# Block 0 through two weight pairs first, x kept on chip, norms as whole sums, and a shorter conversion of float64 words

## Chip, cores and metric

The kernel runs on one core of a Trainium2 chip. The metric is the device time of one execution in microseconds; the median of three runs of the kernel before is 1621.31 us (1619.83 to 1624.52).

## What is computed

Attention over 32 packed queries, a second attention of the queries over that result, and then two gated two-layer MLPs on the 4608 tokens:

```python
def _attn_ref(q, k, v, p):            # q, k, v: 8 x 8 x 576 x 64, p: 8 x 8 x 32 x 64, float32
    p_packed = sm_attn(p, k, v)       # softmax(scale * p k^T) v
    return sm_attn(q, p_packed, p_packed)

def _moe_ref(x, w_gate, w_val, w_out):    # x: 4608 x 512; 512 x 1536 twice, 1536 x 512, float64
    g = x @ w_gate
    return (g * (1.0 / (1.0 + np.exp(-g))) * (x @ w_val) @ w_out).astype(np.float32)

def _moe2_ref(x, w_in, w_out):            # 512 x 2048, 2048 x 512, float64
    h = x @ w_in
    g = np.where(h >= 1, h, np.where(h <= -1, 0.0, (h + 1) ** 2 / 4))
    return (g @ w_out).astype(np.float32)
```

## The kernel before

**Order of the work.** Every operation is handed to a planner (`Order`, lines 43 to 249) with a cost for each engine that can do it, what it reads and writes, and a due time. The planner plays the five engines and one DMA channel through and emits the instructions in the order in which it starts them: it gives each free engine the waiting operation with the earliest due time, and takes TensorE's work from a window of 32 in program order. So costs and due times that are changed at one place move instructions everywhere. DMAs are all issued on the SyncE queue. Buffers come from pools (38 "op" tiles, 4 "raw", 4 "h", 8 PSUM banks "ps" and others); most are handed out in the order in which they were asked for.

**Attention.** Two pairs of heads make a "quad", two quads a batch of 576 tokens, 16 quads in all. `load` (658) and `load_q` (678) bring the inputs; `stage_a` (705) makes the first scores (L697) and their exponentials (L718), `stage_b` (728) the packed result (L741, L760, L788) and its norm, which goes over the partitions with two small matmuls (L799, L807); `stage_c` (832) does the second softmax, and `stage_d` (876) the outputs (L886), which are scaled out of PSUM with a copy (L378 or L382) into an "op" tile and sent to `xT` in HBM.

**Weights.** They are float64. `from_words` (419) turns 512 of them into float32: one ScalarE pass over the upper words (L427), and on VectorE a mask that keeps the sign (L430), a merge of it with the lower words (L434) and a join (L438). `convert_w1` (595) and `prepare_w1` (622) do this for the first MLP, take squares (L391, L393), sum them over the partitions with a matmul against ones (L637) and reduce to the largest (L642); the result is the power of two by which the weights are scaled before they are split into two float16 parts (`split_quarters`, 501; sums and differences on L364). `convert_chunk` (1132) and `prepare_w2` (1175) do the same for the second MLP (L1154, L1161) and keep its weights in HBM in between.

**The MLPs.** Nine blocks of 512 tokens. A unit (`first_unit`, 1392) is the first product of one block with one pair of 128 hidden columns: seven steps of 12 matmuls with 256 columns (L1110). Its second product is added up per block (`second_products`, L1248, for the first three pairs, 24 matmuls of 512 columns to a pair; `second_strassen`, L1366, else). `PHASES` (532) sets which blocks go through which pairs in turn, and `block_x` (1576) where x of a block comes from: for a pair other than the first it is read back from HBM (`fetch_x`, 1218), for the first it is loaded (`load_x`, 1187), scaled and split (`split_x`, 1207). Block 0 needs batch 0 alone (quads 0 and 1), block 1 batches 0 and 1 (quads 0 to 3). `LATE`, `NEXT` and `SPACE` (903 to 905) place the conversions and the quads between the units, two places to a unit.

Of the kernel before, what the change touches and what calls it, by code (L numbers as in the profile page):

```python
# [20 lines left out]
SIGN = -0x80000000  # L21
# [21 lines left out]
class Order:  # L43
# [8 lines left out]
    PATIENCE = {"exp": 0.0}  # L52
    WINDOW = 32
# [72 lines left out]
    def run(self):  # L126
# [34 lines left out]
        def start(op, eng):  # L161
# [9 lines left out]
            else:  # L171
                end = now + op.costs[eng]
# [8 lines left out]
        while issued < len(self.ops) or finishing:  # L181
# [71 lines left out]
def packed_attention_then_two_mlps(ctx, tc, qT, kT, v, pT, w1, wo, w2, wo2, out):  # L253
# [52 lines left out]
    a2s = const.tile([128, 2 * U2], I32, name="a2s")  # L306
    top1 = const.tile([128, U1 + G1], F32, name="top1")
# [5 lines left out]
    kp = const.tile([128, B * NQUAD, 3], I32, name="kp")  # L313
# [105 lines left out]
    def from_words(words, dst, r, w, n):  # L419
# [3 lines left out]

        def bits():
# [76 lines left out]
    def split_quarters(raw, scale, op, key, left, wait_sum=0.0, wait_lo=0.0):  # L501
        base = lambda: raw.t[:, 0:4, :]
        copy(1024, base, base, q(raw, 0, 1, 2, 3) + [key], q(raw, 0, 1, 2, 3), scale=scale)
# [14 lines left out]
    def sums(raw, left, wait):  # L518
# [14 lines left out]
        (1, (0, 1), (0, 2)), (1, (1, 2), (0, 2)), (1, (2, 3), (0, 2)), (1, (0, 3), (2, NB)), (1, (3, 6), (0, NB)),  # L533
# [60 lines left out]

    def convert_w1(item):
# [3 lines left out]
        for src in srcs:  # L599
# [5 lines left out]
            for a, b in ((0, 512), (512, 1024)):  # L605
# [11 lines left out]
                from_words(words, dst, [(wb, 0)], q(raw, *range(a // N, (b - 1) // N + 1)), n)  # L617
# [4 lines left out]
    def prepare_w1(item):  # L622
        kind, p = item
        raws = st.pop(("w1", item))
        ps = o.buf("ps")

        def norm():
            for u, (_, sq) in enumerate(raws):
                s = sq()
                if kind == "out":  # L630
                    moving, dst = [s[:, 0:4:3, :], s[:, 1:3, :]], ps.t
                else:
                    moving = [m[:, :, h:h + 128] for m in (s[:, 0:4:3, :], s[:, 1:3, :])
                              for h in (0, 128)]
                    dst = ps.t[:, u * 256:u * 256 + 256]
                for m, mv in enumerate(moving):
                    nc.tensor.matmul(dst, ones, mv, start=(m == 0), stop=(m == len(moving) - 1))  # L637

        pe(0.43 * len(raws), norm, [k for raw, _ in raws for k in q(raw, 4, 5)], [(ps, 0)],
           unit=ps, opens=True)  # L640
        i = p if kind == "in" else U1 + p
        dve(512, lambda: nc.vector.tensor_reduce(top1[:, i:i + 1], ps.t[:, :512], axis=AX.X, op=ALU.max),  # L642
            [(ps, 0)], [("top", 1, i)], 1.5, 0.0)
# [14 lines left out]
    def load(i):  # L658
        b, qd = divmod(i, NQUAD)
        pb = o.buf("pb")  # L660
        kt, vt = [o.buf("op") for _ in range(2)], [o.buf("op") for _ in range(2)]
# [7 lines left out]
        for j, c0, c1 in ((0, 0, 3), (1, 3, 4)):  # L669
            dma(0.2, lambda j=j, c0=c0, c1=c1: flat(vt[j], (c1 - c0) * 4 * D).rearrange(  # L670
                "p (c d) -> p c d", d=4 * D
            ), lambda c0=c0, c1=c1: v[b, 128 * c0:128 * c1, cols].rearrange("(c p) d -> p c d", p=128),
                [], [(vt[j], 0)])
        dma(0.1, lambda: flat(vt[1], 8 * D)[:S - 512, 4 * D:], lambda: v[b, 512:, cols],
            [], [(vt[1], 1)])
        st["in", i] = (kt, vt, pb)
# [28 lines left out]
    def stage_a(i):  # L705
        kt, vt, pb = st["in", i]
# [22 lines left out]
    def stage_b(i):  # L729
        b, qd = divmod(i, NQUAD)  # L730
        vt = st.pop(("in", i))[1]
# [24 lines left out]
        def values():  # L756
            for c, (off, n) in enumerate(CH):
                vc = flat(vt[c // 3], 768)[:n, (c % 3) * 4 * D:]
# [6 lines left out]
        pe(0.92, values, [(a1T, 0), (a1T, 1), (vt[0], 0), (vt[1], 0), (vt[1], 1)], [(pv, 0)],  # L765
# [58 lines left out]
        if qd == NQUAD - 1:  # L824
# [4 lines left out]
            field(lambda: kx1[:, b:b + 1], lambda: topx[:, b:b + 1], [("topx", b)], [("kx1", b)], 2.0)  # L829
        st[i] = (pp, parts, ppT)  # L830

    def stage_c(i):
# [33 lines left out]
        z2 = o.buf("op")  # L866
# [4 lines left out]
        copy(S, lambda: halves(0), lambda: flat(z, S), [(z, 0)], [(z2, 0)])  # L871
# [4 lines left out]
    def stage_d(i):  # L876
        b, qd = divmod(i, NQUAD)
        pp, parts, z2, halves = st.pop(i)
        for j in range(2):
            xs = o.buf("op")  # L880
            for u in range(2):
# [813 lines left out]
```

## Time and profile before

| | before |
|---|---|
| median of three runs | 1621.31 us |
| the profiled execution | 1620.46 us |
| its span | 1618.7 us |
| TensorE busy | 1555.6 us (96%) |
| VectorE busy | 1298.2 us (80%) |
| GpSimd busy | 1167.4 us (72%) |
| ScalarE busy | 989.4 us (61%) |
| mean granted clock of TensorE | 0.984 |

The span is the part of the execution that the trace covers; 1.8 us lie around it. Busy time is the union of an engine's instructions. A busy TensorE is not one at its peak, since the ends of matmuls are modelled; how many matmuls went into a time tells more. The granted clock is the share of TensorE's higher level, 2.4 GHz.

### The profile page before, as it was taken

How to read it: one execution, taken by the hardware profiler on the slowest of the kernel's cores; microseconds unless marked ns; L12 is line 12 of the kernel's file. 1: busy time of each engine (PE TensorE's matmuls, PEld its weight loads, DVE VectorE, ACT ScalarE, POOL GpSimd, SP SyncE). 2: the span in 40 equal slices, each digit the busy share in tenths (PEclk: the TensorE clock that was granted, in tenths of full speed). 3: DMA queues.
4: the chain of work that ended last, by engine and by line, in shares of the span. 5: the costliest groups of instructions: out<-in, count | busy, mean ns of one | idle time of the engine just before them, and what ended most of it. 6: DMA issues, size and time to landing. Idle time of an engine off the chain costs nothing.

```text
span 1618.7 us, 35291 instructions
## 1 busy us (share of the span) xinstructions
PE 1555.6 (96%) x13772; PEld 1290.2 (80%) x13772; DVE 1298.2 (80%) x2104; ACT 989.4 (61%) x1690; POOL 1167.4 (72%) x993
## 2 busy tenths in 40 slices
PE   4778999999999999999999999999999999999999
PEld 2446666776777778888888888888888888888888
DVE  8889998778675647889999899988777898775674
ACT  5767677677665456666666767666554556654541
POOL 5476556475464357778769989988788888886884
PEclk8779999999999999999999999999999999999999
DMA  8776967647337755666776853245433553244422
GB/s 295 244 268 234 334 223 238 199 170 236 133 140 250 265 179 194 233 249 234 262 238 207 303 190 128 102 150 189 160 105 121 186 182 119 102 170 160 150 60 79
DMA packets 147240, 310.86 MB, mean 192 GB/s; under 512 B 18560, under 2 KB 55424, under 8 KB 147072
## 3 DMA queue, kind: packets, MB, share of 16 engines
q1 hardware_dynamic: 147072, 308.60, 55.7%
q8 instruction: 108, 1.77, 0.4%
q14 instruction: 60, 0.49, 0.1%
HBM read 191.76 MB, written 115.74 MB: 190 GB/s over the span
## 4 chain that ended last, share of the span: by engine, by line
PE 85%; DVE 7%; ACT 2%; issue 2%; POOL 2%; DMA 1%; SPq 0%; POOLq 0%; DVEq 0%; ACTq 0%
PE ps L1110 46%; PE ps L1366 27%; PE ps L1248 7%; PE ps L697 2%; PE ps L886 1%; POOL op L364 1%; POOL raw L364 1%; DVE raw L364 1%; DVE raw L438 1%; DVE h L434 1%; DVE ps L1093 0%; ACT op L376 0%; DMA x2T<-acc 0%; DVE h L1093 0%; PE ps L637 0%
## 5 line engine op out<-in xcount | busy, mean ns | idle before, releaser
L1110 PE MATMUL ps<-op,op 128*128 128x256 f16 x7560 | 906.2, 273 | 7.0 <-DVE u L382 2.5
L1110 PEld LDWEIGHTS <-op 128*128 128x128 f16 x7560 | 737.7, 98 | 116.6 <-issue 14.5
L364 POOL TENSOR_TENSOR op<-h,op 128x512 f16<-128x512 f32 (+2 forms) x344 | 419.5, 1238 | 167.0 <-ACT op L376 140.6
L1366 PE MATMUL ps<-op,op 128*128 128x256 f16 x4158 | 513.3, 273 | 0.0
L1366 PEld LDWEIGHTS <-op 128*128 128x128 f16 x4158 | 406.7, 98 | 47.5 <-issue 0.3
L376 ACT CAST op<-h 128x512 f16<-128x512 f32 (+2 forms) x368 | 202.9, 591 | 92.0 <-POOL h L364 36.1
L364 POOL TENSOR_TENSOR raw<-raw 128x256 f32<-128x256 f32 (+1 forms) x169 | 156.2, 938 | 71.0 <-ACT raw L378 43.4
L364 POOL TENSOR_TENSOR h<-h,h 128x512 f32<-128x512 f32 (+1 forms) x160 | 197.9, 1237 | 11.9 <-DVE h L1488 4.3
L1485 ACT ACTIVATE ps<-m,half,f 128x512 f32<-128x512 f32 x144 | 112.3, 780 | 108.0 <-POOL m L1482 61.1
L378 ACT ACTIVATE p<-ps,f 128x512 f32<-128x512 f32 x174 | 118.8, 685 | 95.2 <-PE ps L1110 90.2
L1266 DVE SCALAR_TENSOR_TENSOR acc<-ps,f,acc 128x512 f32<-128x512 f32 x169 | 125.7, 744 | 58.6 <-PE ps L1366 55.8
L364 POOL TENSOR_TENSOR op<-raw,op 128x512 f16<-128x512 f32 (+3 forms) x100 | 157.3, 1593 | 15.7 <-ACT op L376 9.5
L1248 PE MATMUL ps<-op,op 128*128 128x512 f16 x648 | 155.4, 379 | 0.0
L1488 DVE SCALAR_TENSOR_TENSOR h<-ps,f,h 128x512 f32<-128x512 f32 x144 | 106.4, 742 | 32.5 <-ACT ps L1485 32.3
L1093 DVE SCALAR_TENSOR_TENSOR h<-ps,f,p 128x512 f32<-128x512 f32 x126 | 93.5, 743 | 42.5 <-PE ps L1110 37.2
L1248 PEld LDWEIGHTS <-op 128*128 128x128 f16 x648 | 63.0, 98 | 57.2 <-issue 0.9
L364 POOL TENSOR_TENSOR h<-h 128x512 f32<-128x512 f32 x57 | 78.1, 1371 | 26.0 <-DVE h L1457 15.3
L1482 POOL TENSOR_SCALAR m<-h,f 128x512 f32<-128x512 f32 x72 | 61.7, 856 | 48.6 <-ACT ps L1485 28.9
L364 DVE TENSOR_TENSOR op<-h,op 128x512 f16<-128x512 f32 (+1 forms) x79 | 96.7, 1234 | 0.0
L364 POOL TENSOR_TENSOR op<-op,t 128x576 f32<-128x576 f32 x32 | 39.9, 1246 | 71.9 <-DVE t L848 22.5
L378 ACT ACTIVATE u<-ps,f 128x512 f32<-128x512 f32 x87 | 59.6, 685 | 44.9 <-PE ps L1110 44.6
L376 ACT CAST op<-raw 128x512 f16<-128x512 f32 (+3 forms) x126 | 77.5, 655 | 13.9 <-DVE raw L364 6.9
(148 smaller groups left out, 1791.2 us busy)
## 6 DMA issues: line engine op xcount, KB each, us to landing
op<-xsp SPq DMA_DIRECT2D x88, 448.0 KB, 6.2
xsp<-op SPq DMA_DIRECT2D x72, 448.0 KB, 4.2
sums<-acc SPq DMA_DIRECT2D x88, 256.0 KB, 2.7
acc<-sums SPq DMA_DIRECT2D x88, 256.0 KB, 3.6
op<-wsp SPq DMA_DIRECT2D x44, 448.0 KB, 4.8
op<-wsp_out SPq DMA_DIRECT2D x38, 448.0 KB, 5.3
h<-in_w SPq DMA_DIRECT2D x24, 512.0 KB, 5.2
op<-in_kT SPq DMA_DIRECT2D x32, 288.0 KB, 5.3
```

What stands on the lines that cost most here:

```text
L364: lambda e: engine(e).tensor_tensor(dst(), x(), y(), op=op), r, w, late,
L376: nc.scalar.copy(dst(), src())
L378: nc.scalar.activation(dst(), src(), AF.Copy, scale=scale())
L697: nc.tensor.matmul(ps.t[64 * j:64 * j + 64, :H2], left(j), flat(right[j], S)[:, u * H2:(u + 1) * H2])
L1093: psum_dve(T, lambda: nc.vector.scalar_tensor_tensor(dst(), lanes(bank.t), self.r(), lanes(add.t), op0=ALU.mult, op1=ALU.add), [(bank, 0), ...
L1110: nc.tensor.matmul(dst, a, b, start=start, stop=stop, skip_group_check=True)
L1248: nc.tensor.matmul(bank.t, x[:, js], y, start=first and i == 0 and m == 0, stop=last and i == 1 and m == 2,)
L1266: psum_dve(T, lambda: nc.vector.scalar_tensor_tensor(acc.t, bank.t, pw.output()(), acc.t, op0=ALU.mult, op1=ALU.add), r + [(acc, 0)], [(ac ...
L1366: nc.tensor.matmul(bank.t[:, l * N:(l + 1) * N], x, y, start=first and l == 0 and m == 0, stop=last and l == 1 and m == 2, skip_group_chec ...
L1482: o.add({"POOL": 0.85, "DVE": 0.42}, lambda e: engine(e).tensor_scalar(out=lanes(m.t), in0=dst(), scalar1=top(), scalar2=low(), op0=ALU.mi ...
L1485: act(T, lambda: nc.scalar.activation(bank.t, m.t, AF.Square, bias=half_one[:, 0:1], scale=inv()), [(m, 0), (f, 0)], [(bank, 0)], fixed=0.35)
L1488: psum_dve(T, lambda: nc.vector.scalar_tensor_tensor(dst(), lanes(bank.t), top(), dst(), op0=ALU.mult, op1=ALU.max), [(bank, 0), (h, t), ( ...
```

## The change

`PHASES`: the two first blocks go through pairs 0 and 1 one after the other, block 0 first, where both went through pair 0 and then both through pair 1. `block_x` gives a later one of the first three pairs the x operands that the block had for pair 0, where it read them back from HBM.

x of block 0: `stage_d` writes the outputs of the first 512 tokens, scaled for the MLP, into the "raw" tiles on which `split_x` works; the scale is the new fourth column of `kp`, made when both quads of the batch have their norms. Only the last 64 tokens of batch 0 go to `xT`. The copy by DMA and the scaling pass are left out for this block.

`from_words`: the ScalarE function becomes one with two slopes, which leaves the sign in an exponent bit; VectorE shifts the result left by three and joins the lower words.

Norms of the output weights: ScalarE squares with an accumulated sum (`squares`), a small matmul adds up (`sum_of`).

`load` puts the values beside the keys (three "op" tiles in place of four, four DMAs for the values in place of three), and `stage_c` writes the halves of its result over the tile that it has read. The planner issues no DMA while its model of the channel is more than 4 us behind, counts TensorE's work before 140 us 1.18 times, and puts VectorE work marked "shared" off while the port is taken. `LATE` and `NEXT` change, and x of the next part is asked for one unit ahead instead of two for the first three units.

```diff
@@ class Order
+    QUEUED = 4.0
+    EARLY = 140.0, 1.18
+    PORT, AHEAD = 0.1, 5.0
-                end = now + op.costs[eng]
+                end = now + op.costs[eng] * (self.EARLY[1] if eng == "PE" and now < self.EARLY[0] else 1.0)
-                skipped = []
+                if eng == "SP" and channel - now > self.QUEUED:
+                    upcoming.append(channel - self.QUEUED)
+                    continue
+                skipped, second = [], None
...
+                    if second and op.late > second.late + self.AHEAD:
+                        skipped.append(item)
+                        break
...
-                        start(op, eng)
-                        break
+                        if eng == "DVE" and op.shared and port - now > self.PORT:
+                            second = second or op
+                        else:
+                            second = None
+                            start(op, eng)
+                            break
                     skipped.append(item)
+                if second:
+                    start(second, eng)
@@ def from_words
-            dst(), words()[:, :, 1].bitcast(F32), AF.Abs, scale=2.0 ** -112
+            dst(), words()[:, :, 1].bitcast(F32), AF.Prelu, scale=2.0 ** -112, alpha=-2.0 ** 32
         ), r, w, fixed=0.12)
         dve(n // 2, lambda: nc.vector.tensor_scalar(
-            out=words()[:, :, 1], in0=words()[:, :, 1], scalar1=SIGN, scalar2=None,
-            op0=ALU.bitwise_and,
-        ), r, r, fixed=0.0, shared=True)
+            out=bits(), in0=bits(), scalar1=3, scalar2=None, op0=ALU.logical_shift_left,
+        ), w, w, fixed=0.0, shared=True)
         dve(n, lambda: nc.vector.scalar_tensor_tensor(
-            words()[:, :, 0], words()[:, :, 0], 29, words()[:, :, 1],
-            op0=ALU.logical_shift_right, op1=ALU.bitwise_or,
-        ), r, r, fixed=0.06, shared=True)
-        dve(n, lambda: nc.vector.scalar_tensor_tensor(
-            bits(), bits(), 3, words()[:, :, 0], op0=ALU.logical_shift_left, op1=ALU.bitwise_or,
+            bits(), words()[:, :, 0], 29, bits(), op0=ALU.logical_shift_right, op1=ALU.bitwise_or,
         ), r + w, w, fixed=0.06, shared=True)
@@ PHASES
-        (1, (0, 1), (0, 2)), (1, (1, 2), (0, 2)), (1, (2, 3), (0, 2)), (1, (0, 3), (2, NB)), (1, (3, 6), (0, NB)),
+        (1, (0, 1), (0, 1)), (1, (1, 2), (0, 1)), (1, (0, 1), (1, 2)), (1, (1, 2), (1, 2)), (1, (2, 3), (0, 2)), (1, (0, 3), (2, NB)), (1, (3, 6), (0, NB)),
@@ norms
+    def squares(src, keys, acc, key):
+        act(512, lambda: nc.scalar.activation(junk, src(), AF.Square, accum_out=acc), keys, [key], fixed=0.25)
+    def sum_of(cols, keys, dst, key):
+        t, n = o.buf("ps"), cols.shape[-1]
+        pe(0.1, lambda: nc.tensor.matmul(t.t[:, :n], ones32, cols), keys, [(t, 0)], unit=t, opens=True)
+        dve(n, lambda: nc.vector.tensor_reduce(dst, t.t[:, :n], axis=AX.X, op=ALU.add),
+            [(t, 0)], [key], 1.5, 0.0)
...
+        if kind == "out":
+            sum_of(sq1[:, p, :], [("sq1", p, m) for m in range(2)], top1[:, i:i + 1], ("top", 1, i))
@@ stage_b
+            if b == 0:
+                power(lambda: kpx, lambda: kx1[:, 0:1], -1.0, 202.0, [("kx1", 0)], [("kpx", 0)], 2.0)
+                dve(NQUAD, lambda: nc.vector.tensor_scalar_mul(
+                    kp[:, :NQUAD, 3].bitcast(F32), kp[:, :NQUAD, 2].bitcast(F32), kpx.bitcast(F32)
+                ), [("kpx", 0), *(("kp", j, 2) for j in range(NQUAD))],
+                    [("kp", j, 3) for j in range(NQUAD)], 2.0, 0.0)
@@ stage_d
+            if b == 0:
+                raw = st.setdefault(("x", j), o.buf("raw") if qd == 0 else None)
+                line = lambda raw=raw: raw.t[:, 2 * qd:2 * qd + 2, :].rearrange("p a n -> p (a n)")
...
+                if b == 0:
+                    n = min(hi, T) - lo
+                    copy(n, lambda line=line, lo=lo, n=n: line()[:, lo:lo + n],
+                         lambda xo=xo, n=n: xo.t[:, :n], [(xo, 0), ("kp", i, 3)],
+                         q(raw, *range(2 * qd + u, 2 * qd + 2)), 1.0,
+                         scale=lambda: kp[:, i, 3:4].bitcast(F32), psum=True)
+                    lo = max(lo, T)
@@ places
-    LATE = (1, 2, 5, 6, 14, 26, 38, 43, 48, 52)
+    LATE = (0, 0.5, 5, 7, 14, 26, 38, 43, 48, 52)
-    NEXT, SPACE, AHEAD = (0, 0.5, 1.2, 3.4, 6, 8.5, 11), 2.8, 1
+    NEXT, SPACE, AHEAD = (0.2, 0.9, 1.9, 3.9, 6, 8.5, 11), 2.8, 1
@@ split_x, block_x
-            split_quarters(raw, pw.x(), op, (pw.f, 0), False, SUM_WAIT, X_LO)
+            scale = None if layer == 1 and b == 0 else pw.x()
+            split_quarters(raw, scale, op, (pw.f, 0), False, SUM_WAIT, X_LO)
...
+            if (layer, b, (0, 1)) in xops and pairs[0] < PLAIN:
+                xops[key] = xops[layer, b, (0, 1)]
-            elif pairs[0] > 0:
...
-                if k + 2 < len(line):
-                    block_x(*parts[line[k + 2][0]])
+                then = k + (1 if k < NEAR else 2)
+                if then < len(line):
+                    block_x(*parts[line[then][0]])
```

## Rows read from the trace of the kernel before

**Rows 1.** Busy tenths in 40 slices of 40.5 us; PEclk is the granted clock.

```profile
PE   4778999999999999999999999999999999999999
PEclk8779999999999999999999999999999999999999
```

**Rows 2.** Stages: length, busy us of PE, PEld, DVE, ACT, POOL, clock, DMA share, GB/s.

```profile
0.00:70.60 70.60, 37.32 (x303) 19.75 (x303) 57.20 (x184) 43.16 (x92) 39.19 (x40) 0.76 0.77 258
70.60:114.80 44.20, 33.68 (x276) 21.64 (x275) 36.54 (x92) 31.02 (x61) 27.24 (x23) 0.81 0.82 278
114.80:140.00 25.20, 21.64 (x189) 18.08 (x188) 24.00 (x40) 15.94 (x24) 12.50 (x9) 0.98 0.75 268
140.00:260.00 120.00, 113.22 (x1032) 81.68 (x1031) 113.04 (x239) 89.59 (x165) 77.37 (x64) 1.00 0.79 264
260.00:600.00 340.00, 337.58 (x2706) 244.16 (x2705) 233.86 (x412) 213.72 (x361) 181.42 (x152) 1.00 0.58 197
600.00:1619.00 1019.00, 1012.18 (x9276) 904.84 (x9273) 833.51 (x1140) 595.97 (x993) 829.70 (x708) 1.00 0.50 172
```

**Rows 3.** Chain of waits, first 140 us: start us, us, what.

```profile
23.83 0.61 DVE h L434
...
26.54 1.44 DVE h L434
```

**Rows 4.** ScalarE in order of time: start, us, instruction, [idle before <-releaser].

```profile
51.17 0.50 ACT L378 ACTIVATE op<-ps,kp 128x288 f32<-128x288 f32 x1 [0.22 <-PE ps L886]
...
53.57 0.52 ACT L378 ACTIVATE op<-ps,kp 128x288 f32<-128x288 f32 x1
...
56.93 1.15 ACT L378 ACTIVATE raw<-raw,f 128x1024 f32<-128x1024 f32 x1 [0.17 <-DMA raw<-op]
...
60.89 1.15 ACT L378 ACTIVATE raw<-raw,f 128x1024 f32<-128x1024 f32 x1
```

**Rows 5.** GpSimd in order of time, the same columns.

```profile
58.34 2.88 POOL L364 TENSOR_TENSOR raw<-raw 128x512 f32<-128x512 f32 x3
```

**Rows 6.** TensorE in order of time, the same columns.

```profile
33.59 0.58 PE L807 MATMUL ps<-t,ones 1*128 1x1 f32 x2 [4.12 <-DVE t L805]
...
37.31 0.40 PE L886 MATMUL ps<-op,op 128*128 128x288 f16 x1 [2.17 <-ACT op L376]
...
70.59 5.72 PE L1110 MATMUL ps<-op,op 128*128 128x256 f16 x48
...
79.21 4.09 PE L1110 MATMUL ps<-op,op 128*128 128x256 f16 x36
...
96.57 5.35 PE L1248 MATMUL ps<-op,op 128*128 128x512 f16 x24
...
114.80 11.16 PE L1110 MATMUL ps<-op,op 128*128 128x256 f16 x96
```

**Rows 7.** Instruction groups of the first 140 us: busy, mean ns | idle before.

```profile
L434 DVE SCALAR_TENSOR_TENSOR h<-h 128x512 int32<-128x512 int32 x18 | 16.4, 917 | 0.1
L438 DVE SCALAR_TENSOR_TENSOR raw<-raw,h 128x512 int32<-128x512 int32 x16 | 15.0, 956 | 0.1
...
L430 DVE TENSOR_SCALAR h<-h 128x512 int32<-128x512 int32 x18 | 8.0, 453 | 3.4 <-ACT raw L427 3.3
```

**Rows 8.** Instruction groups of the whole span, the same columns.

```profile
L1439 ACT ACT_TABLE_LOAD x16 | 20.5, 1283 | 0.3
...
L1154 PE MATMUL ps<-raw,ones 128*128 128x512 bf16 x16 | 6.1, 379 | 0.1
...
L1384 PE MATMUL ps<-sq,ones 128*128 128x4 f32 x18 | 2.6, 218 | 0.8 <-ACT junk L1331 0.8
...
L427 ACT ACT_TABLE_LOAD x1 | 1.3, 1283 | 0.7 <-PEq L1684 0.7
```

**Rows 9.** Chain of waits, its last long piece: start us, us, what.

```profile
1586.08 28.83 PE ps L1366 x264
```

**Rows 10.** DMA issues: count, KB each, median us from issue to landing.

```profile
op<-xsp SPq DMA_DIRECT2D x88, 448.0 KB, 6.2
```

More of the change, by code (lines that the diff above doesn't have):

```diff
@@ L501, in split_quarters @@
     def split_quarters(raw, scale, op, key, left, wait_sum=0.0, wait_lo=0.0):
-        base = lambda: raw.t[:, 0:4, :]
-        copy(1024, base, base, q(raw, 0, 1, 2, 3) + [key], q(raw, 0, 1, 2, 3), scale=scale)
+        if scale is not None:
+            base = lambda: raw.t[:, 0:4, :]
+            copy(1024, base, base, q(raw, 0, 1, 2, 3) + [key], q(raw, 0, 1, 2, 3), scale=scale)
         sums(raw, left, wait_sum)
@@ L616, in convert_w1 @@
                 dst = lambda a=a, b=b, line=line: line()[:, a:b]
-                from_words(words, dst, [(wb, 0)], q(raw, *range(a // N, (b - 1) // N + 1)), n)
+                keys = q(raw, *range(a // N, (b - 1) // N + 1))
+                from_words(words, dst, [(wb, 0)], keys, n)
+                if kind == "out":
+                    squares(dst, keys, sq1[:, p, a // n:a // n + 1], ("sq1", p, a // n))
+            if kind == "out":
+                st["w1", item].append((raw, None))
+                continue
             sq = lambda raw=raw: raw.t[:, 4:6, :].bitcast(BF16).rearrange("p a (b n) -> p (a b) n", b=2)
@@ L624, in prepare_w1, with norm @@
         raws = st.pop(("w1", item))
[L625 to L640, printed above, removed]
-        i = p if kind == "in" else U1 + p
-        dve(512, lambda: nc.vector.tensor_reduce(top1[:, i:i + 1], ps.t[:, :512], axis=AX.X, op=ALU.max),
-            [(ps, 0)], [("top", 1, i)], 1.5, 0.0)
+        i = p if kind == "in" else U1 + p
+        if kind == "out":
+            sum_of(sq1[:, p, :], [("sq1", p, m) for m in range(2)], top1[:, i:i + 1], ("top", 1, i))
+        else:
+            ps = o.buf("ps")
+            def norm():
+                for u, (_, sq) in enumerate(raws):
+                    s = sq()
+                    moving = [m[:, :, h:h + 128] for m in (s[:, 0:4:3, :], s[:, 1:3, :]) for h in (0, 128)]
+                    for m, mv in enumerate(moving):
+                        nc.tensor.matmul(ps.t[:, u * 256:u * 256 + 256], ones, mv, start=(m == 0), stop=(m == 3))
+            pe(0.43 * len(raws), norm, [k for raw, _ in raws for k in q(raw, 4, 5)], [(ps, 0)],
+               unit=ps, opens=True)
+            dve(512, lambda: nc.vector.tensor_reduce(top1[:, i:i + 1], ps.t[:, :512], axis=AX.X, op=ALU.max),
+                [(ps, 0)], [("top", 1, i)], 1.5, 0.0)
         field(lambda: k1[:, i:i + 1], lambda: top1[:, i:i + 1], [("top", 1, i)], [("k", 1, i)])
@@ L660, in load @@
         pb = o.buf("pb")
-        kt, vt = [o.buf("op") for _ in range(2)], [o.buf("op") for _ in range(2)]
+        kt = [o.buf("op") for _ in range(3)]
         first = b * NPAIR + 2 * qd
@@ L1146, in convert_chunk, with norm @@
         from_words(words, dst, q(b, "w"), q(b, "d"), 512)
-        square(512, sq, dst, q(b, "d"), q(b, "w"))
+        if i < U2:
+            square(512, sq, dst, q(b, "d"), q(b, "w"))
+        else:
+            squares(dst, q(b, "d"), sqw2[:, i - U2, h:h + 1], ("sq2w", i, h))
         dma(0.25, lambda: w2f[:, i, 512 * h:512 * h + 512], dst, q(b, "d"), [("w2f", i, h)])
-        t = o.buf("ps")
-        n = 128 if i < U2 else 512
-        def norm():
-            for m in range(512 // n):
-                nc.tensor.matmul(
-                    t.t[:, :n], ones, sq()[:, m * n:(m + 1) * n],
-                    start=(m == 0), stop=(m == 512 // n - 1),
-                )
-        pe(0.25, norm, q(b, "w"), q(t, 0), unit=t, opens=True)
-        dve(n, lambda: nc.vector.tensor_reduce(
-            top2[:, i, h:h + 1], t.t[:, :n], axis=AX.X, op=ALU.max
-        ), q(t, 0), [("top", 2, i, h)], 1.5, 0.0)
+        if i < U2:
+            t = o.buf("ps")
+            def norm():
+                for m in range(4):
+                    nc.tensor.matmul(
+                        t.t[:, :128], ones, sq()[:, m * 128:(m + 1) * 128], start=(m == 0), stop=(m == 3),
+                    )
+            pe(0.25, norm, q(b, "w"), q(t, 0), unit=t, opens=True)
+            dve(128, lambda: nc.vector.tensor_reduce(
+                top2[:, i, h:h + 1], t.t[:, :128], axis=AX.X, op=ALU.max
+            ), q(t, 0), [("top", 2, i, h)], 1.5, 0.0)
         if h == 1 and i % 2 == 1:
             j = i - 1
-            dve(1, lambda: nc.vector.tensor_reduce(
-                top2[:, j, 0:1], top2[:, j:j + 2, :], axis=AX.XY, op=ALU.max
-            ), [("top", 2, j + u, c) for u in range(2) for c in range(2)], [("top", 2, j, 0)], None, 0.0)
+            if i < U2:
+                dve(1, lambda: nc.vector.tensor_reduce(
+                    top2[:, j, 0:1], top2[:, j:j + 2, :], axis=AX.XY, op=ALU.max
+                ), [("top", 2, j + u, c) for u in range(2) for c in range(2)], [("top", 2, j, 0)], None, 0.0)
+            else:
+                sum_of(sqw2[:, j - U2:i - U2 + 1, :].rearrange("p a b -> p (a b)"),
+                       [("sq2w", j + u, c) for u in range(2) for c in range(2)], top2[:, j, 0:1],
+                       ("top", 2, j, 0))
             field(lambda: k2[:, j:j + 1], lambda: top2[:, j, 0:1], [("top", 2, j, 0)], [("k", 2, j)])
@@ L1188, in load_x @@
         src = {1: xT, 2: x2T}[layer]
+        if layer == 1 and b == 0:
+            return [st.pop(("x", j)) for j in range(2)]
         raws = []
@@ L1193, in load_x @@
                 halves = lambda kk=kk, kh=kh: src[:, kk + 2 * kh, b * T:(b + 1) * T]
-                if layer == 1 and b == 0:
-                    xs = st.pop(("xs", kh, kk))
-                    halves, r = lambda xs=xs: flat(xs, S)[:, :T], [(xs, 0), (xs, 1)]
-                elif layer == 2:
+                if layer == 2:
                     r = [("x2", b, i) for i in range(4)]
@@ L1382, in total @@
     def total(b):
[L1383 to L1389 removed]
+        sum_of(sq2[:, b, :], [("sq2", b)], topx[:, B + b:B + b + 1], ("topx2", b))
         field(lambda: kx2[:, b:b + 1], lambda: topx[:, B + b:B + b + 1], [("topx2", b)], [("kx2", b)])
```

63 lines of the change are left out of this document (34 added, 29 removed).

## The prediction, made before the change was run

> **What bounds the kernel now.** I read the page's slices first. TensorE is at nine tenths or more from the fifth slice to the end; only the first four, some 160 us, are thin, and there the granted clock is at 0.7 to 0.9 too [rows 1]. So I cut the span into stages [rows 2]. From 600 us on, TensorE is busy 1012.2 of 1019 us. That this is full pace and not only "busy" the end of the chain of waits shows: 264 matmuls of 256 columns in 28.83 us, 109 ns each [rows 9]. In 260 to 600 us it is idle 2.4 us, in 140 to 260 us 6.8 us. Against that it is idle 33.3 of the first 70.6 us, 10.5 of the next 44.2 and 3.6 of the next 25.2, at granted clocks of 0.76, 0.81 and 0.98; from 140 us the mean is 1.00, the higher level of 2.4 GHz [rows 2]. So about 47 of the 63 us of idle time, and all of the slow clock, lie before 140 us. A stage at 0.76 loses on its work too: if the missing part were all time at 1.2 GHz, 37 us of busy time held some 28 us of work.
>
> In that start the other engines set the pace: VectorE is busy 57.2, 36.5 and 24.0 us of these three stages, 118 of 140 in all [rows 2]. The next question is for what the first matmul of the two MLPs waits. It runs at 70.6 us; the first unit (84 matmuls: block 0, pair 0) is done at 83.3, its second product runs at 96.6, and the second unit (block 1, pair 0) starts only at 114.8 [rows 6]. Before the first unit the path is attention quads 0 and 1, then x of block 0. Its last two output copies end at 51.7 and 54.1 us for what becomes the two x tiles; each tile then goes through a DMA and a scaling pass, which start at 56.9 and 60.9 us [rows 4], and the first sums start on GpSimd at 58.3 [rows 5]; those of the second tile can't before its pass ends, 62.0. Before 31.5 us the conversion of weights lies on VectorE in the middle of the same chain [rows 3].
>
> **The change part by part.**
>
> *x kept on chip.* The copies out of PSUM write x, already scaled, into the tile that the sums read. Gone before the first unit are the copying DMAs and two passes of 1.15 us. Taken from the same copies, the sums could start at 51.8 and 54.2 instead of 58.3 and 62.0: 6.5 to 8 us on the path. Added are two VectorE instructions of one and two columns for the scale and a short copy for each tail, and a new wait: quad 0's copies now want the norm of quad 1. In before that norm's broadcast runs at 33.6 us and quad 0's first output matmul at 37.3 [rows 6], so the wait should end first and nothing queue behind it. I take 6 us, since GpSimd and VectorE have quad 2's softmax to do in the same stretch; bounds 3 and 8.
>
> *Conversion of words.* For each 512 weights VectorE now does a shift and a join where it did a mask, a merge and a join. The shift is a one-input instruction on 512 words like the mask (453 ns), the join is like the old one (956), so the merge is what goes: 917 ns, and there are 18 before 140 us, 16.4 us of VectorE time [rows 7]. ScalarE's part stays one pass. What of it is on the path? Two merges stand in the chain at 23.8 and 26.5 us with 2.05 us [rows 3]; the others shorten VectorE's list, which is full in this stretch. I take 2 us for the first unit, bounds 1 and 4.
>
> *Block 0 through two pairs first.* The second unit then needs the weights of pair 1 in place of attention quads 2 and 3 and x of block 1. A unit is 9.2 us of TensorE at full pace (84 x 109 ns) and its second product 24 x 218 ns = 5.2 us, so some 14 us of work that needs no attention become available in a stage that is idle for 10.5 us and then for another 3.6 [rows 2, 6]. The work of VectorE, ScalarE and GpSimd is only moved, however, and the weights of pair 1 have to be split earlier than now. I take 7 us, half of the 14.1 that are idle; bounds 0 (they limit as before) and 12. A denser TensorE should also see the clock at its higher level sooner; that is inside the upper bound, not added. Of the reads of stored x, 16 of 448 KB go for the first two blocks (two blocks, two later pairs, four halves); no idle time of TensorE from 70 us on that I cost is put down to them, so 0. If the cover were gone, each would be worth its 6.2 us to land [rows 10].
>
> *Whole norm sums.* For the output weights the matmul of 512 columns against ones goes: 16 for the second layer and, two for each of six matrices, 12 for the first. By 109 ns for 256 columns each holds TensorE for 0.22 us, 6.1 us in all [rows 8, 9]. Ten small sums come in their place; the 18 matmuls of the same form that exist take 218 ns each, two to a sum, so 2.2 us if they pipeline and 4.4 if not. Most lie where TensorE is full, so the difference counts in full: 1.7 to 3.9 us, I take 3. The squares go to ScalarE alone; at 596 of 1019 us busy [rows 2] it hides them.
>
> *The rest.* Idle time from 140 to 600 us is 9.2 us; lighter conversions can free some, I take 1, bounds 0 and 4. The planner's new rules (transfers held back, work marked shared put off, a dearer TensorE early) move nearly every instruction without adding work. From 600 us on there are 6.8 us of idle time to win; to lose there is more. I take 0, bounds 2 gained and 3 lost.
>
> The sum is 6 + 2 + 7 + 3 + 1 = 19 us. The profiled execution took 1620.46 us (span 1618.7 and 1.8 around it), 0.85 below the median of the three runs. 1620.5 - 19 = 1601.5, and on the median's footing 1602. The ends of the bounds: 3 + 1 + 0 + 1.7 + 0 - 3 = 2.7 us gained, 1618; 8 + 4 + 12 + 3.9 + 4 + 2 = 33.9, 1587.
>
> **A rule against the row.** In before, table loads of 1283 ns stand ahead of the silu passes [rows 8] and the exponentials, while the old conversion (an absolute value) runs between them without one of its own but the first. The Trainium skill, "ScalarE: Activation LUTs", section "Table sets: the hidden batching unit", says that cheap functions (it names relu, copy, identity and abs) are in every set, and that a function which is not costs a load; the two-slope function is not in its list, and no run here shows it. If it is filler like the others, the sum stands; if not, the rival of the table comes.
>
> **The rivals.**
>
> *The other engines limit as before.* The order brings nothing, because the weights of pair 1 are split no sooner than quads 2 and 3 were done: 12 us remain, 1609. For it: VectorE is busy 36.5 of 44.2 us between the two units. Against it: the merges that go free some 16 us of just that engine.
>
> *Given back.* Block 1 comes with its attention later, and the stall that closes at 83 us opens again ahead of its first unit, or in 140 to 260 us, where VectorE is busy 113 of 120 us [rows 2]. The two x operands of two blocks, 8 of 38 "op" buffers, stay taken through three pairs, so loads of attention find buffers later. The 7 us go, and some 8 of the first unit's lead are waited out again: 3 us remain (the norm sums), 1618.
>
> *The table.* The two-slope function is in neither the exp nor the silu set. Each run of conversions between softmax work then costs two loads, 2.57 us of ScalarE, in a start where ScalarE is busy 43 of 70.6 us and hands the copies to the path. With 18 conversions before 140 us, about two to a run, that is nine pairs or 23 us, against 19 gained: 1624, and more if runs are single. It decides from the eighth pair on the path (19 / 2.57 = 7.4); fewer eat the gain only. For it nothing but the absence from the trace; against it, three other cheap functions (absolute value, square, copy) need no load.
>
> *The plan.* The SyncE queue holds transfers back until the modelled channel is 4 us from free. If the real queue is faster, fetched weights land late in the full stretch; each late one costs up to 6.2 us [rows 10]. With the gain of 19, five would make it slower, 1632. Before has slack there: TensorE waits for hardly anything after 260 us.
>
> **How the numbers follow.** A measurement of this kernel can tell about 0.3%, 5 us, from no change. My forecast, 1602, with 1590 to 1608 for its own range: 0.58. The engines limit, 1609: 0.20. Given back, 1618: 0.12. The table, 1624: 0.06. The plan, 1632: 0.04. So faster 0.78, within 0.3% 0.12, slower 0.10. The range goes from the lower end of the bounds, 1587, to 1618, which leaves out half of the given-back case, the two slower ones and a little below, about 0.2.
>
> **What would show it.** Right: the first 256-column matmul of the MLPs at about 62 us in place of 70.6, no scaling pass or DMA between the last output copies and the sums of x, the second unit within about 20 us of the first one's end, 16 fewer reads of stored x, one wide instruction less for each conversion, no table load at the conversion's line beyond the first, TensorE idle some 30 us in the first 140 instead of 47, and the same full pace from 260 us on. Wrong: table loads between conversions, a new gap of over 10 us ahead of block 1, idle time beyond 5 us in the full stretch, or conversions that take as long as before because their remaining instructions stretch (in the chain one merge stands with 0.61 us and the next with 1.44 [rows 3]).

## The result, and the profile after

The changed kernel takes 1602.22 us (median of four runs, 1601.51 to 1602.78) against 1620.57 for the kernel before beside it: a ratio of 0.9883, 95% interval 0.9864 to 0.9901. That is 18 us, and the forecast was 1602. The profiled execution took 1602.37 us, its span is 1600.6. The sum came out; several of its terms did not come about as the prediction put them, and the runs below show it.

The stages of the changed kernel, with the columns of [rows 2]:

```profile
0.00:70.60 70.60, 38.88 (x327) 24.07 (x328) 54.93 (x184) 46.22 (x101) 41.32 (x42) 0.85 0.76 251
70.60:114.80 44.20, 32.96 (x321) 22.01 (x321) 41.25 (x98) 34.60 (x71) 31.54 (x25) 0.91 0.69 229
114.80:140.00 25.20, 24.36 (x176) 16.93 (x175) 19.94 (x40) 15.51 (x30) 19.65 (x19) 0.96 0.56 191
140.00:260.00 120.00, 115.77 (x1064) 84.56 (x1064) 99.02 (x224) 91.77 (x174) 68.38 (x55) 1.00 0.75 248
260.00:600.00 340.00, 338.35 (x2754) 249.65 (x2753) 226.66 (x390) 209.19 (x364) 185.55 (x160) 1.00 0.57 195
```

TensorE is idle 31.7, 11.2 and 0.8 us in the first three stages, 43.8 in all, where before had 33.3, 10.5 and 3.6 [rows 2]. That is only 3.6 us less. What rose is the granted clock of the first two: 0.85, 0.91 and 0.96 for 0.76, 0.81 and 0.98. Busy time by clock, summed over the three stages, is 76.9 us at full pace before (37.32 x 0.76 + 33.68 x 0.81 + 21.64 x 0.98) and 86.4 after. So TensorE is some 9.6 us further at 140 us; as a sum, about 3 of it are less idle time and 6 shorter matmuls at the higher level. That is bookkeeping: it doesn't say that the clock caused the gain, and the run that fills a wait, below, speaks against it. A second count agrees on the advance. TensorE's matmuls of the MLPs in the first 140 us and the next 120 (first the line of the 256-column product, then that of 512 columns; columns: length, PE busy, PEld busy, clock, DMA share, GB/s), of before:

```profile
0.00:140.00 140.00, 29.32 (x252) 24.82 (x252) 0.82 0.78 266
140.00:260.00 120.00, 62.36 (x528) 50.91 (x528) 1.00 0.79 264
...
0.00:140.00 140.00, 5.35 (x24) 2.27 (x24) 0.82 0.78 266
140.00:260.00 120.00, 27.87 (x120) 11.67 (x120) 1.00 0.79 264
```

and of the changed kernel:

```profile
0.00:140.00 140.00, 34.03 (x276) 27.21 (x277) 0.89 0.70 233
140.00:260.00 120.00, 65.37 (x556) 53.51 (x556) 1.00 0.75 248
...
0.00:140.00 140.00, 13.12 (x54) 5.29 (x54) 0.89 0.70 233
140.00:260.00 120.00, 25.76 (x108) 10.50 (x108) 1.00 0.75 248
```

At 109 ns and twice that, 32.7 us of work before and 41.9 after lie ahead of 140 us, 9.2 more; in the next stage 83.7 and 84.1.

The start of the units in the changed kernel, TensorE in order of time:

```profile
59.36 1.99 PE L1170 MATMUL ps<-op,op 128*128 128x256 f16 x16
61.97 6.51 PE L1170 MATMUL ps<-op,op 128*128 128x256 f16 x56 [0.62 <-POOL op L384]
...
71.30 1.47 PE L1170 MATMUL ps<-op,op 128*128 128x256 f16 x12 [1.64 <-DVE k L460]
...
87.10 2.65 PE L1170 MATMUL ps<-op,op 128*128 128x256 f16 x12
...
95.03 1.46 PE L1314 MATMUL ps<-op,op 128*128 128x512 f16 x6
```

The first unit begins at 59.4 us, not 70.6 [rows 6], its long run at 62.0, and it is done at 72.8; the second, now block 0 with pair 1, begins 14.3 us later (31.5 before). Between the last output copies, which end near 53.4 us, and the sums of x there is no scaling pass and no DMA: GpSimd has

```profile
52.74 2.41 POOL L384 TENSOR_TENSOR raw<-raw 128x512 f32<-128x512 f32 x2 [3.49 <-ACT raw L398]
```

The conversion of words and the table loads (groups of the whole span, but the first two lines, which are of the first 140 us):

```profile
L454 DVE SCALAR_TENSOR_TENSOR raw<-h,raw 128x512 int32<-128x512 int32 x18 | 14.3, 804 | 0.2
L451 DVE TENSOR_SCALAR raw<-raw 128x512 int32<-128x512 int32 x18 | 9.9, 554 | 7.8 <-ACT raw L448 7.7
...
L1499 ACT ACT_TABLE_LOAD x15 | 19.2, 1283 | 1.5 <-DVE ps L1153 1.2
...
L448 ACT ACT_TABLE_LOAD x1 | 1.3, 1283 | 0.7 <-PEq L1747 0.7
```

A conversion is a shift and a join now, with means of 554 and 804 ns (the mask had 453, the join 956 [rows 7]); the merge is gone. One load stands at the conversion's line, as before [rows 8]. Reads of stored x are 72 in place of 88 [rows 10]:

```profile
op<-xsp SPq DMA_DIRECT2D x72, 448.0 KB, 6.3
```

### The profile page after: what moved, and what is told of

The parts are those of the page before. It is cut to its first block, busy times and chain, and to the rows that moved or that the text cites. A ratio compares the mean times of both kernels' runs of the same rounds, so it can differ in the third digit from the quotient of the medians.

```text
span 1600.6 us, 35182 instructions
## 1 busy us (share of the span) xinstructions
PE 1544.3 (96%) x13764; PEld 1287.5 (80%) x13764; DVE 1245.8 (78%) x2023; ACT 982.6 (61%) x1719; POOL 1156.8 (72%) x997
## 4 chain that ended last, share of the span: by engine, by line
PE 86%; DVE 6%; ACT 2%; issue 1%; POOL 1%; DMA 1%; SPq 0%; DVEq 0%; POOLq 0%; ACTq 0%
PE ps L1170 47%; PE ps L1432 27%; PE ps L1314 8%; PE ps L735 1%; PE ps L936 1%; POOL op L384 1%; DVE op L384 1%; DVE raw L384 1%; DMA h<-in_w 1%; DVE h L1153 1%; ACT op L396 0%; DVE raw L454 0%; PE ps L798 0%; SPq L426 0%; POOL raw L384 0%
## 5 line engine op out<-in xcount | busy, mean ns | idle before, releaser
L384 POOL TENSOR_TENSOR h<-h,h 128x512 f32<-128x512 f32 (+1 forms) x157 | 191.5, 1220 | 9.4 <-DVE op L384 3.7
L1542 POOL TENSOR_SCALAR m<-h,f 128x512 f32<-128x512 f32 x79 | 66.1, 837 | 50.2 <-ACT ps L1545 32.4
L384 DVE TENSOR_TENSOR op<-h,op 128x512 f16<-128x512 f32 x75 | 86.9, 1167 | 2.1 <-POOL h L384 1.1
L1153 DVE SCALAR_TENSOR_TENSOR ps<-ps,f,u 128x512 f32<-128x512 f32 x54 | 40.7, 755 | 60.5 <-PE ps L1170 52.7
L396 ACT CAST op<-raw 128x512 f16<-128x512 f32 (+3 forms) x125 | 78.5, 669 | 11.2 <-POOL raw L384 8.5
```

The costliest lines, as they stand in the source:

```text
L384: lambda e: engine(e).tensor_tensor(dst(), x(), y(), op=op), r, w, late,
L396: nc.scalar.copy(dst(), src())
L1153: psum_dve(T, lambda: nc.vector.scalar_tensor_tensor(dst(), lanes(bank.t), self.r(), lanes(add.t), op0=ALU.mult, op1=ALU.add), [(bank, 0), ...
L1542: o.add({"POOL": 0.85, "DVE": 0.42}, lambda e: engine(e).tensor_scalar(out=lanes(m.t), in0=dst(), scalar1=top(), scalar2=low(), op0=ALU.mi ...
```

## The experiments

Two kinds were run. In one a part is put back or a rule changed, and the planner then makes a new order for every engine. In the other the changed kernel's plan stays and an operation is made longer where it stands. All times are medians beside runs of the kernel before on the same chip (1620.4 to 1621.0); ratios are to these.

**Parts put back, one at a time.** Each part is the old text in the changed kernel, as it stands with a minus in the diff.

The order (old `PHASES`, `LATE`, `NEXT`, and `NEAR = 0`):

> The changed kernel with the order of the parts undone alone: both first blocks through pair 0 and then both through pair 1, the places of conversions and quads as before, x asked for two units ahead. Everything else stays changed. My theory (the order is worth 7 us): 1609 us, 7 slower than the changed kernel's 1602.2, and a gap of 10 us or more between the first unit and block 1. Rival (the other engines limit, the order is worth nothing): 1602 to 1604. Rival (the order carries nearly all, through a TensorE that is kept dense and so at its higher clock): 1615 or more.

Measured 1612.85 us (ratio 0.9946, 0.9931 to 0.9961). Its first stages:

```profile
0.00:70.60 70.60, 37.28 (x297) 20.60 (x298) 52.83 (x180) 42.29 (x97) 38.25 (x39) 0.74 0.74 243
70.60:114.80 44.20, 32.11 (x267) 20.57 (x265) 38.23 (x84) 32.63 (x61) 29.28 (x26) 0.81 0.61 208
114.80:140.00 25.20, 24.66 (x192) 19.55 (x191) 16.91 (x39) 18.55 (x35) 8.15 (x8) 0.91 0.49 170
```

Idle time is 33.3, 12.1 and 0.5 us, nearly the changed kernel's; the clock is 0.74, 0.81 and 0.91, below it. Busy by clock is 76.0 us in place of 86.4. Its matmuls of the MLPs ahead of 140 us, counted as above, and its first unit:

```profile
0.00:140.00 140.00, 31.22 (x240) 24.87 (x240) 0.79 0.65 218
...
0.00:140.00 140.00, 9.37 (x36) 3.80 (x37) 0.79 0.65 218
```

```profile
68.31 2.77 PE L1170 MATMUL ps<-op,op 128*128 128x256 f16 x12
...
80.22 4.09 PE L1170 MATMUL ps<-op,op 128*128 128x256 f16 x36
```

That is 34.0 us of work in place of 41.9: the order's gain is in the start. The first unit begins only at 68.3 us and is done at 84.3 (83.3 before), although x is kept on chip here and GpSimd starts its sums at 53.1 us, as early as in the changed kernel (52.7); attention matmuls stand ahead of the unit on TensorE.

The old conversion:

> The changed kernel with the old conversion of words (absolute value, mask, merge, join) alone. My theory: 2 us for the first unit and 1 later, so 1605. Rival (VectorE's list sets the pace of the whole start, so that 16 us of merges before 140 us count nearly in full): 1612 or more. Rival (hidden, since VectorE waits for other things): 1602.

Measured 1603.61 us (0.9896, 0.9878 to 0.9913), and its first unit begins earlier than the changed kernel's:

```profile
54.69 0.61 PE L1174 MATMUL ps<-op,op 128*128 128x256 f16 x4
55.61 6.55 PE L1174 MATMUL ps<-op,op 128*128 128x256 f16 x56 [0.32 <-POOL op L384]
```

By the median that is 1.4 us, nearly hidden, but its runs go from 1602.9 to 1608.2, and the profiled one took 1606.8. See the same instructions at a fixed plan, below.

x of block 0 the old way (`stage_d`, `load_x` and `split_x` of before):

> The changed kernel with x of block 0 taken the old way alone: output copies into a buffer, a DMA into the tile and a scaling pass. My theory: the first 256-column matmul of the MLPs comes 6 us later, about 65 instead of 59.4, and the time is 1608. Rival (the DMA and the pass lie beside quad 2's softmax, which limits): first matmul within 2 us of 59.4 and 1602 to 1604.

Measured 1615.84 us (0.9966, 0.9955 to 0.9977). Its first unit waits for x on the way:

```profile
62.30 0.37 PE L1156 MATMUL ps<-op,op 128*128 128x256 f16 x1 [4.86 <-ACT op L396]
...
66.09 0.80 PE L1156 MATMUL ps<-op,op 128*128 128x256 f16 x3 [3.42 <-POOL op L384]
...
68.82 7.84 PE L1156 MATMUL ps<-op,op 128*128 128x256 f16 x56 [1.93 <-DVE op L384]
```

The long run of 56 stands at 68.8 us in place of 62.0, 6.9 later: the expected 6. The time lost twice that.

The old norms:

> The changed kernel with the old norms of the output weights alone (squares in two-byte floats, matmuls of 512 columns against ones, a maximum). My theory: 3 us more TensorE work in the full stretch, 1605. Rival (the matmuls filled idle places of TensorE): 1602. In both cases the start up to 140 us is about the same.

Measured 1610.46 us (0.993, 0.9916 to 0.9944), 8 us where 3 were expected.

These four lose 34 us together, and there were 18 to lose. Some of that is overlap: the order put back and x put back each take most of the first unit's lead. How much is the planner's choice of an order, the next runs tell. Two parts of the change were not put back by themselves, the new places of the values and of the second softmax's result, and the x operands kept for later pairs; what they are worth is open.

**The plan by itself.** One modelled cost of the changed kernel is moved by one hundredth:

```diff
-    EARLY = 140.0, 1.18
+    EARLY = 140.0, 1.17
```

> The changed kernel with a modelled cost that says nothing new: TensorE before 140 us is counted 1.17 times in place of 1.18. No work changes, the plan does. It measures how far a new plan alone moves the time, and so what the other comparisons can tell: my expectation is a shift of at most 3 us from 1602.2, with the first unit within 2 us of 59.4. Rival (the plan was fitted so closely that any other costs more): 1606 to 1612, which would account for the half of what each part put back has cost beyond its own price.

Measured 1609.13 us (0.9926, 0.9912 to 0.9939): 6.9 us from nothing but another order. Its stage from 140 to 260 us:

```profile
140.00:260.00 120.00, 110.87 (x1017) 81.66 (x1016) 97.17 (x215) 86.46 (x166) 69.36 (x59) 0.99 0.73 245
```

Five us more idle time than the changed kernel has there, with no more work on VectorE and ScalarE. The three rules of the planner switched off:

```diff
-    QUEUED = 4.0
+    QUEUED = 1e9
-    EARLY = 140.0, 1.18
-    PORT, AHEAD = 0.1, 5.0
+    EARLY = 140.0, 1.0
+    PORT, AHEAD = 1e9, 5.0
```

> The changed kernel with the planner's new rules switched off (no limit on modelled queued DMAs, TensorE not dearer early, no putting off of shared work); all work is as in the changed kernel. My theory: within 3 us of 1602.2. Rival (the rules carry a good part of the gain, by sending DMAs in a better order or by keeping VectorE off the port): 1607 or more.

Measured 1610.12 us (0.9939, 0.9927 to 0.9951). The rival's number, but not its proof: the new plan of the run above cost as much with the rules on. And the kernel before, with a delay moved by a thousandth of a microsecond:

```diff
-    LAG = 0.12
+    LAG = 0.121
```

> The kernel before with a modelled delay that says nothing new (0.121 us in place of 0.12 from an operation's end to what it releases). No work changes, the plan does. After the changed kernel lost 7 us to such a new plan, this tells how closely before's plan was fitted. My theory (both are about equally fitted, so the 18 us between the kernels are the change's): 1625 to 1630. Rival (before's plan is an ordinary one): 1618 to 1623, and then a good part of the 18 us is the choice of one plan among many.

Measured 1625.82 us (1.0027, 1.0014 to 1.004): 4.8 us. So either kernel moves by 5 to 8 us with its plan. The changed work took 1602.2, 1609.1 and 1610.1 us under three plans, and 1605.8 under a fourth (below), 1606.8 on the mean; the old work 1620.6 and 1625.8, 1623.2 on the mean. The slowest of the four is 10 us below the faster of the two. The change is worth some 16 us by these means, of few plans each, and what one part put back costs can't be told from its plan to better than about 7 us. The place of the first unit can: its long run stands at 62.4 and 62.6 us under the first two of the other plans, 62.0 in the changed kernel.

**The first DMAs.** In the changed kernel the weights' DMAs go out behind the first keys, and the first conversion starts at 8.1 us instead of 4.8. Put back in front:

```diff
-                    [], [(wb, 0)])
+                    [], [(wb, 0)], -20.0 if item == ("in", 0) else None)
```

> The changed kernel with one due time moved: the four DMAs of the first weights are due first, so that they go out ahead of the first keys, as in the kernel before. In the changed kernel the first conversion starts at 8.1 us instead of 4.8 (the shorter chain of the conversion gives its DMA a later due time), and the old conversion put back alone started its first unit at 54.7 us instead of 59.4. My theory (this is why the shorter conversion brought nothing before 70 us): the first conversion starts at about 4.8, the first 256-column matmul at 55 or earlier, and the time is 1598 to 1600. Rival (the start of the conversion is not on the path; other instructions moved): first matmul within 1 us of 59.4 and 1602.

Measured 1605.83 us (0.9905, 0.9891 to 0.9918). ScalarE and TensorE:

```profile
4.35 0.66 ACT L448 ACTIVATE raw<-h 128x512 f32<-128x512 f32 x1 [2.33 <-DMA h<-in_w]
```

```profile
56.38 0.61 PE L1170 MATMUL ps<-op,op 128*128 128x256 f16 x4
58.31 6.27 PE L1170 MATMUL ps<-op,op 128*128 128x256 f16 x56 [1.32 <-POOL op L384]
```

The mechanism is there: the first conversion begins 3.8 us earlier, the first unit 3.0, its long run 3.7. The time was not: the plan behind it has 114.1 us of TensorE in 140 to 260, where the changed kernel has 115.8, and the lead is gone by 300 us.

**The order alone, in the kernel before** (`PHASES`, `LATE`, `NEXT` and the earlier request for x; x is still read back for the second pair):

> The kernel before with the order of the parts alone changed (parts, places, and x asked for one unit ahead in the first three units); x of block 0 by DMA, old conversion, old norms, old planner, stored x read back for later pairs. My theory: 6 to 11 us faster than before's 1621, so 1610 to 1615. Rival (the order needs the other parts to bring anything, since the engines beside TensorE limit the start): 1618 to 1622.

Measured 1631.17 us (1.0062, 1.005 to 1.0075), slower than before. Its matmuls of the MLPs, with the lines and columns of the two counts above:

```profile
0.00:140.00 140.00, 33.60 (x244) 25.84 (x245) 0.84 0.77 264
140.00:260.00 120.00, 60.85 (x511) 49.92 (x509) 0.96 0.74 252
...
0.00:140.00 140.00, 11.50 (x48) 4.69 (x48) 0.84 0.77 264
140.00:260.00 120.00, 24.32 (x96) 9.30 (x96) 0.96 0.74 252
```

37.1 us of work ahead of 140 us, 4.4 more than before; 76.6 in the next stage, 7.1 less. The order does bring work forward, and more than that is missing again by 260 us. The long run of the first unit comes 7.3 us earlier than in the kernel before (70.6), with x still by DMA and a scaling pass:

```profile
63.28 8.47 PE L1110 MATMUL ps<-op,op 128*128 128x256 f16 x56 [1.90 <-POOL op L364]
```

Some of the 10.8 us may be its plan, which the run can't separate.

**At the changed kernel's own plan.** Each join is done twice (the second changes nothing):

```diff
-        dve(n, lambda: nc.vector.scalar_tensor_tensor(
-            bits(), words()[:, :, 0], 29, bits(), op0=ALU.logical_shift_right, op1=ALU.bitwise_or,
-        ), r + w, w, fixed=0.06, shared=True)
+        def join():
+            nc.vector.scalar_tensor_tensor(
+                bits(), words()[:, :, 0], 29, bits(), op0=ALU.logical_shift_right, op1=ALU.bitwise_or,
+            )
+
+        dve(n, lambda: [join() for _ in range(2)], r + w, w, fixed=0.06, shared=True)
```

> The changed kernel with its own plan, instruction for instruction, but each join of words done twice in a row (the second changes nothing). It puts 68 wide VectorE instructions of about 0.9 us back, 18 of them before 140 us, where the old conversion had its merges, and leaves the plan alone. My theory (the merges are worth 2 to 4 us, since VectorE's list is full before 140 us but conversions stand off the path): 1604 to 1607. Rival (VectorE sets the pace of the start): 1612 or more. Rival (nothing: the old conversion put back with a new plan differed by 1.4 us only): 1602 to 1603.

Measured 1626.2 us (1.0034, 1.0021 to 1.0046): 24 us, more than the whole change. The first unit starts at 64.7 us. Ahead of 140 us stand 228 matmuls of 256 columns and 36 of 512, 32.7 us of work, as much as in the kernel before: 9.2 of the 24 us, and the whole lead of the start. Most of the rest is far behind the start, where TensorE was full. TensorE's first 256-column matmuls here, then the stage from 600 to 800 us of this kernel and of the changed one:

```profile
64.69 1.99 PE L1173 MATMUL ps<-op,op 128*128 128x256 f16 x16
```

```profile
600.00:800.00 200.00, 193.98 (x1793) 172.86 (x1792) 175.35 (x260) 130.15 (x224) 151.99 (x129) 1.00 0.69 235
```

```profile
600.00:800.00 200.00, 198.94 (x1848) 178.29 (x1846) 163.24 (x252) 137.67 (x243) 153.90 (x135) 1.00 0.75 251
```

An engine that is busy 163 of 200 us has room for 12 more, but not at any place of a fixed order. Under the planner's own order for the old conversion the same work cost 1.4 us (1603.61); whether that order hid it or was a lucky one, the scatter of some 7 us leaves open.

The columns of the old norms, put back as 112 matmuls of 128 against ones:

```diff
-        pe(0.1, lambda: nc.tensor.matmul(t.t[:, :n], ones32, cols), keys, [(t, 0)], unit=t, opens=True)
+        def norm():
+            for _ in range({("sq1"): 8, ("sq2w"): 16}.get(keys[0][0], 0)):
+                nc.tensor.matmul(t.t[:, 128:256], ones, ones, start=True, stop=True)
+            nc.tensor.matmul(t.t[:, :n], ones32, cols)
+
+        pe(0.1, norm, keys, [(t, 0)], unit=t, opens=True)
```

> The changed kernel with its own plan, but TensorE does 112 matmuls of 128 columns against ones ahead of the ten small sums, as many columns as the 28 matmuls of 512 that the change left out. It prices these columns without a new plan. My theory: 28 x 0.22 = 6 us at full pace, less what falls into idle places before 140 us: 1606 to 1609. Rival (they fill idle places): 1602 to 1603.

Measured 1608.64 us (0.9922, 0.9908 to 0.9935), 6.4 us, beside the 6.1 of the sum.

TensorE's wait at 34 us, filled:

```diff
                 def outputs(j=j, u=u, xo=xo):
+                    for _ in range(40 if (i, j, u) == (0, 0, 0) else 0):
+                        nc.tensor.matmul(xo.t[:, :128], ones, ones, start=True, stop=True)
```

> The changed kernel with its own plan, but TensorE does 40 matmuls of 128 columns against ones in the 6 us in which it waits, from 33.7 to 39.9 us, for quad 0's output matmuls to get their operands. In 30 to 50 us the granted clock is at 0.57 and 0.67 after that wait. My theory (the clock falls because TensorE is idle, and costs a microsecond or two of the path to the first unit): the clock of 30 to 50 us at 0.85 or more, the first unit 1 to 2 us earlier, time 1600 to 1602. Rival (the clock there costs nothing, since the other engines set the path): a higher clock and the same time. Rival (the clock does not follow TensorE's idleness): no higher clock and a time of 1602 or more.

Measured 1602.93 us (0.9889, 0.9873 to 0.9905), the same. The clock of 20 to 50 us in steps of ten, first of the changed kernel, then of this one:

```profile
20.00:30.00 10.00, 6.68 (x101) 4.09 (x101) 7.10 (x15) 7.41 (x23) 8.99 (x8) 0.83 0.98 351
30.00:40.00 10.00, 3.13 (x13) 1.61 (x14) 9.93 (x38) 7.15 (x14) 7.25 (x7) 0.57 0.87 291
40.00:50.00 10.00, 5.24 (x25) 2.72 (x24) 10.00 (x19) 5.21 (x14) 8.78 (x6) 0.67 0.86 271
```

```profile
20.00:30.00 10.00, 8.28 (x103) 4.42 (x96) 7.38 (x21) 6.45 (x21) 8.60 (x9) 0.58 1.00 359
30.00:40.00 10.00, 6.86 (x53) 4.78 (x52) 9.92 (x32) 7.24 (x14) 7.00 (x7) 0.67 0.95 309
40.00:50.00 10.00, 6.07 (x27) 3.23 (x27) 10.00 (x22) 5.32 (x14) 8.16 (x6) 0.67 0.69 208
```

TensorE was busy 3.7 us longer in 30 to 40 and the clock after it, in 40 to 50, stayed at 0.67; in 20 to 30, ahead of the fill, it stood lower than in the changed kernel, so it also differs where the order is the same. VectorE is full in these 20 us, so a faster TensorE had nothing to win there either. The run tells more about the stage after it, and about the matmuls of the MLPs:

```profile
70.60:114.80 44.20, 34.01 (x323) 22.71 (x323) 41.12 (x97) 34.48 (x71) 31.40 (x24) 0.83 0.68 231
```

```profile
0.00:140.00 140.00, 34.14 (x276) 27.24 (x277) 0.85 0.70 232
...
0.00:140.00 140.00, 13.12 (x54) 5.29 (x54) 0.85 0.70 232
```

The clock from 70.6 to 114.8 us is 0.83, near the 0.81 of the kernel before and not the changed kernel's 0.91, and yet the matmuls done by 140 us are the same, 276 and 54, and so is the time. TensorE is busy 34.0 us of that stage in place of 33.0: the slower matmuls filled idle time. At this order the higher clock of the stage was worth nothing that shows. Why the clock differs between two kernels of one order is not settled.

## Why the prediction was right, and where its steps were not

**The reading of before was right.** Half of the gain lies ahead of 140 us, 9.2 to 9.6 us. From 140 to 260 us idle time is 4.2 us in place of 6.8 and from 260 to 600 us 1.7 in place of 2.4 [rows 2], 3.3 us together where the sum had 1; the norms' columns, 6.1 us, less the 3.1 us for which TensorE is busy with the ten sums are 3 more. That is some 16 of the 18 us, and from 600 us on the changed kernel is as full as before (6.6 us idle, 6.5 before).

**x kept on chip** was sized at 6 us for the first unit. Its long run came 8.6 us earlier (62.0 for 70.6), and putting x back takes 6.9 of them: right in size, beside the new order. But the sum took it as enough by itself, and it is not: without the order the sums of x began as early and the unit was done no earlier than before. The order alone, with x by DMA, brought the long run to 63.3. The two overlap, and the prediction added them.

**Conversion of words**: "2 us for the first unit" failed. The shorter conversion gave its DMA a later due time, the DMA went behind the keys, and the first conversion began 3.3 us later; with the old conversion the first unit came 4.7 us earlier, not later. Of these, 3.0 came back with the DMAs in front; the rest is open. The prediction costed the merge as time on a chain and did not ask what its absence does to the due times that set the order. Its bounds of 1 to 4 us were not those of a fixed order either: there as much work cost 24.

**Block 0 first**: 7 us were to come out of 14.1 idle. Idle time fell by 3.6 only, and the sign that the prediction named (some 30 us of idle time in the first 140) is wrong: it is 43.8. Counted in work the size was about right, 7.9 us of matmuls ahead of 140 us (10.6 us of time, within the plan's scatter). Idle time was the wrong measure of it: more work came with shorter matmuls, at a higher clock, and the run with the filled wait did as much work at a lower clock and less idle time. The prediction had the clock inside its upper bound; no run shows that the clock gave anything. It also put none of the first unit's lead down to the order, and without the order that unit began at 68.3 us in place of 59.4. That the order in turn stands on the other parts it did not see: alone, it was 10.8 us slower. Which of them it needs most, no run separates.

**Norms**: 6.1 us of columns measured 6.4; less ten small sums, 3 is consistent. Right.

**The plan**: "I take 0, bounds 2 gained and 3 lost" is the step that failed by the most. Another order of the same work is worth 5 to 8 us, as much as any term of the sum. The term should have had bounds of some 8 us to both sides, which would have widened the range to about 1581 to 1623; that the sum met 1602 so closely is in part the luck of one plan.

**The rivals.** "The table" did not come: 30 table loads in place of 32, one at the conversion's line, and the ScalarE pass takes 669 ns. The Trainium skill, "ScalarE: Activation LUTs", section "Table sets: the hidden batching unit", has cheap functions in every set without naming this one; the trace agrees for the two-slope function, which has no load at its line beyond the first. "The plan" did not come: the kernel took 1602 us, not 1632, and without the planner's new rules 1610. Its doubt was sound in another way, since two plans other than the one chosen gave 7 to 8 of the 18 us back. "The other engines limit as before" did not come either, the second unit began 14.3 us after the first; but its reason holds, since the doubled joins on VectorE alone took the start's whole lead. "Given back" is what the order alone did, in the stage that the rival named, 140 to 260 us.

## What to carry to other kernels

Where a planner writes the order, one part put back or added is compared under two plans; move a cost that means nothing first, on both kernels, and take that shift as the least doubt of every single comparison. To price an operation itself, keep the emitted order and make the operation longer or double where it stands. And before an operation is shortened, look at what its length set elsewhere: due times, the order of the first DMAs, and which engine has room at that place.

## What the runs showed of the hardware

The same order of work with 68 more wide VectorE instructions, some 70 us of them on an engine that is busy 1246 of 1601, cost 24 us; VectorE's share of the span says little about what it can take. In the first 140 us idle time of TensorE fell by 3.6 us while its work advanced by 9, at a granted clock of 0.85 and 0.91 in place of 0.76 and 0.81. That does not make the clock the cause: at one order, 0.83 in place of 0.91 from 70.6 to 114.8 us left the matmuls done by 140 us and the time as they were. In such a start, where TensorE waits for other engines, idle time and clock alone mislead; counted matmuls tell how far it is.
